# A gated linear attention and token-mixing kernel with its steps issued in another order

## Chip, cores and metric

The kernel runs on one core of one Trainium2 chip, in one launch. The metric is the device time of that core in microseconds (us), and the median over several runs is what counts.

## What is computed

Gated linear attention (batch 4, 8 heads, 768 tokens, head dimension 48) gives x, and a token-mixing layer with 384 channels follows. All is float32.

```python
f = 1.0 / (1.0 + np.exp(-f_logit))
for t in range(S):
    state = f[:, :, t, :, None] * state + np.einsum('bhd,bhe->bhde', k[:, :, t], v[:, :, t])
    y[:, :, t] = np.einsum('bhd,bhde->bhe', q[:, :, t], state)
x = y.transpose(0, 2, 1, 3).reshape(B, S, H * D)

theta = x @ w_theta
zr, zi = x * np.cos(theta), x * np.sin(theta)
y = np.einsum('ts,bsd->btd', w_tok_r, zr) + np.einsum('ts,bsd->btd', w_tok_i, zi)
u = x + y
out = u + np.maximum(u @ w_ch, 0.0)
```

## The kernel before

The 768 tokens of each batch are cut into 6 chunks of 128, so the attention has 24 chunks (numbered 0 to 23 over all batches). The mixing works on 8 groups: a group is one batch and one half (384) of its output tokens. The weights arrive as 64-bit floats in 16 parts and are decoded to float32 on the chip. For batches 1 to 3 each matrix product of the mixing layer is made of three products of split (high and low) operands; batch 0 uses whole float32 operands.

The work is divided into small steps, each a function that issues a few instructions. `ORDER` is one hand-fixed list of 1169 steps, the engines' programs follow it, and every engine runs its own instructions in that order and waits where an operand or a buffer isn't ready. A step code stands for its next number: the third `gk` in the list is `gk` 2. A mark after a slash sends the step's instruction to another engine than its usual one: /A ScalarE, /D VectorE, /P GpSimd. The loop at L608 to L613 reads the list: it counts each code, sets the engine (L612) and calls the function (L613). Since a list entry is the n-th of its code, chunks, parts and groups are always done in the same sequence among themselves; the list sets only how the codes interleave.

The codes, with their line and engine:

- Loads, all issued from SP: `lf`, `lk`, `lq` (gates, keys, queries of a chunk, L555), `lv` (values, L560), `lw` (raw weights of a part, L202, two transfers for most parts). Three buffers each for f, k, q and v: a load waits until the chunk three before has been used.
- Gates of a chunk: `gc` clamp (VectorE or GpSimd, L269), `go` (ScalarE, L274 and L275), `gs` scan (VectorE, L279), `ge` two exponentials (ScalarE, L286 and L287), `gp` (GpSimd, L290), `gq` scale q (VectorE or GpSimd, L294), `gk` scale k (VectorE, L299).
- Attention of a chunk: `sc` scores (TensorE, L333), `ma` mask (VectorE, L339), `ke` transposes of k (TensorE, L347), `kt` copy (ScalarE or VectorE), `up` state update products (TensorE, L362), `sa` and `st` (VectorE, L370 and L374), `sm` (VectorE or GpSimd, L378), `qs` and `ou` output products (TensorE, L393 and L401), `xc` copy of x, `xt` transposes (TensorE, L411), `xs` copy into the output tile u (ScalarE or VectorE). `sc`, `up`, `qs` and `ou` use 64-row tiles of TensorE, all other TensorE steps 128 rows.
- Angles of a chunk: `xh`, `xl` split x (the second on VectorE or GpSimd, L433), `th` (TensorE, L442), `tn`, `se`, `ab` reduce the angle, `tr` sine and cosine (ScalarE, L465 and L466, with a change of its function table), `ro` rotate (VectorE, L475), `zh`, `zl` split the result (L482).
- Weights of a part: `d1` (VectorE, L215), `d2` (ScalarE, L220), `d3` (VectorE, L225 and L226), `di`, `d4`, `d5` (scale and split, the last L250), `e4`, `e5` the same for the channel weights.
- Mixing: `f0`, `f1`, `f2` are the products of one chunk for a third of the channels (TensorE, L498), `v` adds them to u (VectorE, L502), `uh`, `ul` split u (the second L509), `c` channel products (TensorE, L516), `cv` (VectorE, L530), `so` store (SP, L534). The last group's store stands at L690, behind the list.

`PLACES` names, for each kind of tile, the buffer that its n-th tile takes: `a` the two double banks of PSUM, `b` four single banks, `wp` decoded weights, `z` raw weights and rotated chunks, and so on.

## Time and profile before

| | us |
|---|---|
| median of 3 runs | 337.95 |
| lowest and highest of them | 337.77, 339.97 |
| the profiled execution, its own time | 338.16 |
| its span, from the first to the last instruction | 335.5 |

The profile is of one execution. Engines are PE (TensorE matmul), PEld (its weight loads), DVE (VectorE), ACT (ScalarE), POOL (GpSimd) and SP (which issues the transfers). Ends of matmuls are modelled, so the distance between the first weight loads of two steps tells better what a step takes than the busy time. A wait is named by what released it; "issue" means that the profile shows nothing that the engine waited for.

### The profile page before, as it was taken

To read this page: it belongs to the slowest core of one execution; us is meant where nothing else is said; L and a number is where in the kernel's file an instruction comes from. 1 tells how busy PE (TensorE), PEld (TensorE's weight loads), DVE (VectorE), ACT (ScalarE), POOL (GpSimd) and SP (SyncE) were. 2 spreads that over 40 slices of the span, in tenths; PEclk is the share of its full clock that TensorE was granted. 3 is DMA by queue.
4 is the path that set the end of the run, shared out by engine and by line. 5 is a ranking of instruction groups with operands and counts; after the bars stand their busy time and mean duration, and the time that the engine had idled before them with its cause. 6 is when DMAs were issued, how large, how long until landed. Compare 5 with 4: busy or idle time off the path is not lost.

```text
span 335.5 us, 9996 instructions
## 1 busy us (share of the span) xinstructions
PE 316.8 (94%) x4320; PEld 280.7 (84%) x4320; DVE 243.4 (73%) x394; ACT 192.9 (58%) x321; POOL 112.3 (33%) x109
## 2 busy tenths in 40 slices
PE   0798999999999999999999999999999999999993
PEld 0685676567676789999999999999999999999992
DVE  5999999999999899968659777774526677441031
ACT  6789977787696799847468253953805342310010
POOL 2452074318100146265371248143800521103110
PEclk9999999999999999999999999999999999999998
DMA  7989779758660463240405353250122102000022
GB/s 266 395 244 304 254 249 340 249 181 308 243 212 17 150 225 111 91 156 15 130 3 168 115 160 117 88 178 0 33 73 79 49 2 73 0 2 0 0 73 77
DMA packets 21619, 45.54 MB, mean 136 GB/s; under 512 B 2369, under 2 KB 5441, under 8 KB 21569
## 3 DMA queue, kind: packets, MB, share of 16 engines
q1 hardware_dynamic: 21568, 44.84, 39.6%
q8 instruction: 36, 0.59, 0.7%
q14 instruction: 15, 0.11, 0.1%
HBM read 40.11 MB, written 4.72 MB: 134 GB/s over the span
## 4 chain that ended last, share of the span: by engine, by line
PE 83%; DVE 9%; ACT 2%; DMA 2%; issue 2%; DVEq 0%; ACTq 0%
PE pm L498 47%; PE pch L516 10%; PE pth L442 9%; PE wide L401 4%; PE wide L393 3%; PE wide L333 3%; PE pxt L411 2%; PE psk L347 2%; PE wide L362 2%; DVE f L279 2%; DMA out_dram<-ut 1%; DVE z L475 1%; DVE raw L215 1%; DMA f<-in_f_dram 1%; DVE k L299 1%
## 5 line engine op out<-in xcount | busy, mean ns | idle before, releaser
L498 PE MATMUL pm<-wp,z 128*128 128x384 f32 x648 | 117.1, 336 | 0.0
L498 PEld LDWEIGHTS pm<-wp,z 128*128 128x128 f32 x648 | 112.4, 188 | 0.0
L498 PE MATMUL pm<-value,z 128*128 128x384 f32 x144 | 49.3, 487 | 0.2 <-DVE z L475 0.2
L516 PE MATMUL pch<-uhl,wch 128*128 128x384 f32 x216 | 40.2, 339 | 0.4 <-DVE ut L176 0.4
L498 PEld LDWEIGHTS pm<-value,z 128*128 128x128 f32 x144 | 26.3, 190 | 15.9 <-DVE value L226 0.5
L516 PEld LDWEIGHTS pch<-uhl,wch 128*128 128x128 f32 x216 | 37.5, 188 | 1.0 <-DVE ut L176 0.7
L290 POOL COPY pes<-p 128x4 f32<-128x4 f32 x24 | 11.4, 476 | 72.6 <-ACT p L286 68.2
L502 DVE TENSOR_TENSOR ut<-pm,ut 128x384 f32<-128x384 f32 x24 | 13.1, 552 | 29.8 <-PE pm L498 29.8
L176 ACT CAST uhl<-ut 128x384 fp32r<-128x384 f32 x18 | 9.2, 509 | 41.5 <-DVE ut L502 41.5
L279 DVE TENSOR_TENSOR_SCAN f<-carry,f 128x512 f32<-128x512 f32 x24 | 29.1, 1222 | 0.7 <-ACT f L275 0.7
L433 POOL TENSOR_TENSOR xl<-ut,xh 128x384 fp32r<-128x384 f32 x13 | 13.5, 1041 | 46.1 <-DVE xh L176 29.1
L286 ACT ACTIVATE p<-f 128x512 f32<-128x512 f32 x24 | 15.1, 628 | 21.7 <-DVE f L279 21.3
L509 POOL TENSOR_TENSOR uhl<-ut,uhl 128x384 fp32r<-128x384 f32 x13 | 13.5, 1047 | 37.0 <-DVE uhl L176 18.6
L347 PE MATMUL psk<-ident,k 128*128 128x128 f32 (+1 forms) x96 | 16.8, 302 | 8.9 <-DVE k L299 8.8
L269 POOL TENSOR_SCALAR f<-f 128x512 f32<-128x512 f32 x14 | 23.3, 1668 | 1.5 <-DMA f<-in_f_dram 1.5
L530 DVE SCALAR_TENSOR_TENSOR ut<-pch,ut 128x384 f32<-128x384 f32 x24 | 13.0, 553 | 14.7 <-PE pch L516 14.4
L482 POOL TENSOR_TENSOR z<-w,z 128x768 fp32r<-128x768 f32 x9 | 17.4, 1931 | 17.8 <-ACT z L176 9.6
L442 PE MATMUL pth<-wth,xh 128*128 128x384 f32 x108 | 23.0, 348 | 0.0
L299 DVE SCALAR_TENSOR_TENSOR k<-f,k 128x512 f32<-128x512 f32 x24 | 19.5, 813 | 3.7 <-ACT f L287 3.6
L401 PEld LDWEIGHTS wide<-v,sc 64*64 64x64 f32 x768 | 15.0, 140 | 8.1 <-issue 4.7
L347 PEld LDWEIGHTS psk<-ident,k 128*128 128x128 f32 (+1 forms) x96 | 11.9, 148 | 11.6 <-POOL pes L290 8.8
L475 DVE TENSOR_TENSOR w<-w,x 128x768 f32<-128x768 f32 x18 | 18.1, 1010 | 4.0 <-ACT w L466 4.0
(84 smaller groups left out, 607.3 us busy)
## 6 DMA issues: line engine op xcount, KB each, us to landing
v<-in_v_dram SPq DMA_DIRECT2D x24, 384.0 KB, 4.4
f<-in_f_dram SPq DMA_DIRECT2D x24, 256.0 KB, 3.6
k<-in_k_dram SPq DMA_DIRECT2D x24, 256.0 KB, 4.1
q<-in_q_dram SPq DMA_DIRECT2D x24, 256.0 KB, 3.9
raw<-in_w_r_dram SPq DMA_DIRECT2D x12, 384.0 KB, 5.1
raw<-in_w_i_dram SPq DMA_DIRECT2D x12, 384.0 KB, 5.6
out_dram<-ut SPq DMA_DIRECT2D x21, 192.0 KB, 2.4
raw<-in_w_theta_dram SPq DMA_DIRECT2D x3, 384.0 KB, 5.5
```

The source lines that it names most:

```text
L269: on(nc.vector).tensor_scalar(ft, ft, F_MIN, None, op0=ALU.max)
L279: nc.vector.tensor_tensor_scan(fl, carry[:, pairs(h)].rearrange("p n t -> p (n t)"), fl, 0.0, ALU.mult, ALU.add)
L286: nc.scalar.activation(ps_[m][:, pairs(h)], ft, AF.Exp, scale=-1.0)
L299: nc.vector.scalar_tensor_tensor(kt, loaded["f", m][:, pairs(h)], E_TOP, kt, op0=ALU.min, op1=ALU.mult)
L347: nc.tensor.transpose(psks[m][:used(m), p, :], loaded["k", m][:, p, :used(m)], ident)
L401: nc.tensor.matmul(out[HALF[t], j, p, :], scs[m][HALF[a], j, p, :], v2[HALF[a], t, p, :], start=(t == 0 and m % NC == 0 and p == 0), stop= ...
L433: on(nc.vector).tensor_tensor(xls[m], src, xhs[m], op=ALU.subtract)
L442: nc.tensor.matmul(pths[m], l, r, start=(n == 0), stop=(n == len(ms) - 1))
L475: nc.vector.tensor_tensor(zs[m] if full else w, w, xs[m].unsqueeze(1).to_broadcast([P, 2, DM]), op=ALU.mult)
L482: on(nc.vector).tensor_tensor(zs[m][:, 0], ws[m], zs[m][:, 1], op=ALU.subtract)
L498: nc.tensor.matmul(pms[g, d], l, r, start=(s == 0 and i == 0), stop=(s == NC - 1 and i == len(ms) - 1))
L516: nc.tensor.matmul(pcs[g, d], l, r, start=(es[0] == 0 and n == 0), stop=(es[-1] == KD - 1 and n == len(ms) - 1))
```

## The change

Only two tables change. `ORDER` holds the same 1169 steps, code by code, in another sequence, and some steps carry another engine's mark: on VectorE instead of GpSimd two more `gc`, three `d5`, two `xl`, two `zl` and one `sm`; on GpSimd instead of VectorE one more `gq` and one `ul`; on VectorE instead of ScalarE four `tn`, three `kt`, two `xc`, one each of `d4`, `xs` and `uh`; on ScalarE instead of VectorE two `xh`, two `zh` and two `ab`. In `PLACES` the rows `a`, `b`, `wp` and `z` name other buffers; the other rows stay. The new list in full, and of the old one the first twelve lines, three of the middle and the last six:

```diff
 PLACES = {
-    "a": "0110110101001010110101010101010101010101010101010",
-    "b": ("012301230120123023300300002121123222230230203120310202001031023333312312023011203100000023"
-        "1030303030032123123211120303031"),
+    "a": "0110101010110100101010101010110010101010101010101",
+    "b": ("012301230123103202200200003013121111231231202101201202021230130300000321230121202010102131"
+        "3103213131213021021223100313102"),
     "f": "012012012012012012012012",
     "k": "012012012012012012012012",
     "q": "012012012012012012012012",
     "ut": "01201201",
     "v": "012012012012012012012012",
     "w": "010101010101010101010101",
-    "wp": "0123456789abcdefghijklmno013245687cd",
+    "wp": "0123456789abcdefghijklmno012354689gi",
     "x": "012012012012012012012012",
-    "z": "0123450123412342342350421350421350421",
+    "z": "0123450123512351351430512430512430512",
 }
 ORDER = (
-    "lf gc go lf gc go lf gs lk lq gc gs ge gk gq ke go gp lv sc ge gp gs lk lw lq kt lv lf gk d1 lk lw gq/P lf",
-    "up lq sa d2/P ke kt st ge d3 di d4 qs lv up ma gp ou xc lw sm/P sa gk ke st d1 lf d2 gq gc/P go sm/P d5 gs",
-    "qs gc/P d1 kt lk sc up go sa ma st ge gp gk lq lk d3 lv xt xs lf ou xc gq gs di d2/P gc/P ke kt lq xt go d3",
-    "gs th lw gc ge gp tn se lv gq qs gk sc up ma lq d1 xs go gs sm/P ab/A th ge gq ke kt lk gp ou sa st sm xc xt",
-    "gk d2 xs qs d3 sc up lw ge tr ma tn ro se lv ab gp lq ke kt th tn se sa st ou xc f1 xt xs/D lk qs gk sc tr",
-    "up ma sm/P lf lf d1 ab/A tr ro ro/P ke kt/D gc/P gc/P go sa lv th f0 go gs ou xc gq/P sc up lf gs ma qs sa",
-    "st ge lk gk xt gp f0 d4 f1 tn se xs th lq d2/P lw ke kt d3 sm lk gq/P ou xc/D tn ge se lv d1 sc up ma qs",
-    "d2/P xt f1 f2 f2 xs sa lw gc/P d1 ab ab/A d2 d3 d3 lw d1 f2 lw go gs d5/P th tr ro st tn sm/P gp lv lq gk d1",
-    "gq lq se tr d2 lk f0 ab/A f0 f1 ou ke ro f0 lf tr xc qs d3 kt sc up lw lw d1 xt ro/P f0 d2 d3 d2/P xs f1 f1",
-    "f1 d3 gc/P f1 d1 v lq ge d2 lv go lf xh gp gk gq/P sa st v ke ma xl/P ou sc kt up sm/P gs ge xc/D qs xt sa",
-    "st d4 gc/P xs d4/D f2 d4 ma lk gq lw d1 d2 lf gc/P th tn f2 f2 d3 lw d1 go lq gk ke d3 f1 go gs gs f1 uh kt",
-    "f2 se xh gp ge gq gp lw d1 ou xc ul/P v uh ab xl d2 d3 lv ge gp lk sc up ma qs d2 d3 xt lw xs ul tr f0 f2 f2",
...
-    "sc up xc ma gq qs ke kt/D sa f2 f2 ul uh ul/P f1 f0 ro/P v uh lv ul v c c xh/D cv cv lq c cv zh lf ou xc/D",
-    "sc up v ma gp ge sa qs xl/P uh/D uh gp ul ul gc/P go xt gq xt zl/P lk gk th tn se st ab tr lv sm/P c c so so",
-    "so lf xs/D cv gc/P lk c xh/D xl th zl/P xs xh xl/P ro/P ke kt ou xc/D cv sc up qs xt tn zh/D f0 lv se ab/A",
...
-    "xs so ul kt f2 f2 f2 xh/D xl/P th ma ou ro/P ro/P zh xc sc up ma qs zh/D zl/P tn xt f1 xs se xh/D f1 v sm f2",
-    "v zl/P f1 uh/D ul sa xl/P th ou uh xc tn ab/A gq qs sc xt ma ul/P c xs/D se tr ro/P xh/D xl/P c cv so cv c",
-    "zh/D zl cv ou xc/D th xt xs/D tn/D se ab/A tr f2 ro ab/A f0 f0 gp fl f1 f2 f1 zh tr zl ro/P xh xl/P f0 th tn",
-    "se ab/A zh/D zl tr ro f2 f2 zh zl f0 so f1 f0 f1 f1 f1 f0 v uh/D f1 f2 f1 f1 f1 f2 v f2 so v uh/D uh ul/P f0",
-    "f2 f2 f0 f0 f0 f0 f0 v f2 ul/P ul/P c c cv cv so f1 c cv v so so uh uh f2 f2 v ul/P c ul/P uh ul c c rv cv",
-    "cv cv",
+    "lf lf lf gc gc lk go gs lq gc go lk gs ge gk lq gp ke lv lv gq sc go gs lf ge gk gq/P kt up sa st gp sm ge",
+    "gp ke lk gk kt lw d1 qs lq lf lv gc/P up sa ma st gq/P go lf gs ke d2/P gc kt d3 ou sc xc go gs ge lw gp qs",
+    "di d1 lq d4 lk up lk ma sm/P sa gq/P xt xs/D st d2 gk ge ou xc d3 di lq gq sc ke lw gp lf xt gc/P go d1 d2",
+    "gk gc th lv lf qs kt xs gs d3 up ma ke ge go sm/P sa tn th lk st gk se tn ou lv xc sc xt qs sm kt/D up xs/D",
+    "th gs ma ou ab/A lq gq/P lw d1 gp tr ro lf ge lq sa st lv ke d2/P se xc kt/D tn/D f1 ab/A gc/P gq qs lk gk",
+    "lv gp se sc go up ma xt xs sm f0 ab sa tr tr d3 ro/P lw d1 gs ke ro/P kt th lf ou xc d2 tn d3 sc up sa qs xt",
+    "f1 xs lw lw ge ma lk d1 d1 d2 gc/P go st se th gk lq lq ab/A gq lv f0 gs f1 ou tn/D gp xc ke kt qs sc up",
+    "gc/P ge xt se ab/A sm/P sa d3 f2 f2 f2 lw lf lk tr lw ma lq d1 ro f0 lk d2 d3 d1 gq/P d2/P gk lw xs d4 d4 f0",
+    "th f2 gc/P tr ro/P f2 gp st tn/D d2/P se d5 ab/A tr d1 f1 d3 ke d2 ou kt sc lv up sm/P xc qs xt ro/P f0 f0",
+    "go go f1 xs xh xl/P d3 f1 sa d3 gs ge d5/P f2 ma lw d1 gk ke st lv ou d2 kt v d5 d3 xc sc up qs lq lf sm",
+    "gc/P v lw lf xt xs/D f2 gq gp gs d4 lk lw th tn/D f1 d4 d4 d4/D d4 f1 f2 se ma v d1 ge gp f2 d4 lv lk gc gk",
+    "ke xh/D d1 f0 sa st uh go ou sc gq/P kt gs d2/P lw xc up qs d2/P d3 ma xt xl/P d1 f1 lf d3 ge f2 gc/P xs sm",
+    "sa d2 d5 go gs f0 d3 f1 st lw lq ab lw th tn se tr f0 gk lq f2 d1 ab/A ke xh f0 d2/P tr f1 d1 ro/P gq sc gp",
+    "ul kt d3 d2 d3 ou uh lk ro xl f0 ge gq/P zh zh f1 xc/D f0 gk qs lv lv v uh e4 lf lf up ma sm ke zl/P lq sa v",
+    "e4 e5 e5 go ul/P kt th ou xc uh sc up ul tn se lk lk gs qs ab/A d5 gp c ul/P lv sa tr c c cv f2 st so ro/P",
+    "cv cv gc/P go zl v f1 f1 uh ul so so ge xt gp uh gk ke ma gq ou sc kt xc/D d4/D xs xh/D xl up ma d4/D gs qs",
+    "xt xt zh sm ul/P lf xs th tn se xh xl/P d4/D c d5 ab c sa cv st zl xs ge tr c th gp lq gq tn gk xh f1 cv cv",
+    "se ab/A tr f0 f0 ke ro zh/D zl xl/P ro/P so th tn lv kt/D gc/P gc/P f0 ou xc sc lk up so so se ab/A zh zl qs",
+    "d5 d5/P tr sm/P d5 go go gs ge gs xt lq lf ro/P gq/P zh/D zl/P lv lk xs f2 f2 f2 xh xl ma lq gc f0 gp f1 f1",
+    "f0 f2 f2 sa th tn f0 v se ab ou d4 d5/P ge gq xc f1 gp f2 gk ke uh gk go lf f1 f1 st d5 f1 ul/P v v lf kt/D",
+    "qs sm sc up gc gs xt lk ke kt/D uh uh sa st xs ge xh/D xl/P f2 f2 sm/P f2 ma ul/P gc gk go th tn/D ou d5 tr",
+    "lv ul sc up sa lq se gq d4/D xc qs c f0 cv ab gp f1 gs ro lv st ke so ge kt ma zh lk gk f0 f0 f0 c go gp tr",
+    "ou xc/D sc up cv d5/P zl qs d5 xt xs lq f0 f2 lf xh xl lk lq gq/P gc ma lv go c f0 gs ge so cv so f1 sm/P sa",
+    "gp f1 f2 v uh/D ul/P gq v uh gs gk f2 v uh/D ro/P zh/D th tn xt xs/D ke kt zl/P ou xc/D sc up qs xt se xh xl",
+    "ke kt/D ab/A f2 xs th sa tr st tn/D ul/P ul/P c ge lk c ro cv lf lf gk ma cv f2 zh zl/P se ke ou xh xl sc lq",
+    "gp xc lv up qs xt so th ab tr ro xs f0 f0 f0 tn/D xh xl/P se th kt/D zh zl f0 c lv ma ou sm sa st ab/A tr ro",
+    "zh/D sc up tn se xc/D cv qs ab/A so so ma xt xs/D tr ro/P zh/D lq f1 lq zl/P zl lf f1 f1 gc/P f0 sm f1 f1 f2",
+    "f0 go f0 gc gc gq xh xl/P v gs ge gp f2 f2 f1 v f2 f1 lk gk sa go v th go tn/D f1 ke se st ou gq/P xc/D gs",
+    "sm/P sc kt lv up ma qs sa gs xt xs lk ge gq uh gk st sm/P lq lk gp f1 f0 ul f0 f0 f1 ge gq xh/D f0 uh f0 f1",
+    "uh/D v ul/P ab tr uh lv f1 ke ul kt/D ou xc/D sc up qs xl/P v c cv f2 th sa st gk f2 ro so zh f2 zl/P ke tn",
+    "se xt xs/D ab xh xl/P c sm/P c uh cv so ma ou kt tr lv f2 cv f2 so ro/P qs xc sc up ma xt zh/D zl th tn se",
+    "ou xc f2 sa qs xs xh/D sc v uh/D xt ab/A xl/P tr xs th tn ul/P ul/P se f0 ul/P f0 ro/P zh/D zl/P c xh/D xl",
+    "cv c cv ab/A tr th ma ou tn/D se f2 xc xt f1 xs/D f2 f2 xh xl/P ro/P ab/A tr zh zl th tn/D se ab/A gp f2",
+    "ro/P zh zl tr ro f1 f1 f1 f1 f0 zh zl f0 f0 f2 f2 f0 v f1 v f2 c v f0 so f0 f0 f0 uh/D uh/D fl ul ul f0 f0",
+    "cv f2 v f2 f1 so so f1 uh uh/D f1 f2 f2 f2 ul/P c cv c cv f1 f1 f1 ul c v v c uh uh so so cv so ul c ul/P c",
+    "rv cv cv cv",
```

## Rows read from the trace of the kernel before

**Rows 1.** The page, busy time of each engine (share of the span) and instructions.

```profile
PE 316.8 (94%) x4320; PEld 280.7 (84%) x4320; DVE 243.4 (73%) x394; ACT 192.9 (58%) x321; POOL 112.3 (33%) x109
```

**Rows 2.** Busy time by stretches: start:end, length, each engine, granted clock, DMA share, GB/s.

```profile
45.00:112.00 67.00, 66.88 (x937) 45.22 (x936) 65.77 (x101) 51.46 (x86) 19.81 (x19) 1.00 0.67 233
112.00:330.00 218.00, 217.19 (x2710) 210.57 (x2708) 137.67 (x231) 103.94 (x173) 76.03 (x65) 1.00 0.24 76
```

**Rows 3.** In order of time, 0 to 20 us: start, duration, engine, line, what [idle <-releaser].

```profile
3.63 0.43 DVE L269 TENSOR_SCALAR f<-f 128x512 f32<-128x512 f32 x1 [2.03 <-DMA f<-in_f_dram]
...
4.09 1.08 SPq L202 DMA_DIRECT2D raw<-in_w_theta_dram  x2
...
8.72 0.33 SPq L555 DMA_DIRECT2D f<-in_f_dram  x1
8.80 0.71 PEld L347 LDWEIGHTS psk<-ident,k 128*128 128x128 f32 x4 [8.80 <-POOL pes L290]
```

**Rows 4.** The same, 314 to 336 us.

```profile
324.70 4.70 PEld L516 LDWEIGHTS pch<-uhl,wch 128*128 128x128 f32 x27
...
330.46 0.39 SPq L690 DMA_DIRECT2D out_dram<-ut  x1
```

**Rows 5.** The chain that ended last, in order of time: start, us, what.

```profile
72.03 6.45 PE pm L498 x20
...
160.95 10.41 PE pm L498 x60
171.36 1.56 PE pth L442 x9
...
188.94 4.68 PE pch L516 x27
```

**Rows 6.** In order of time, weight loads (PEld) of 117 to 120 us.

```profile
116.83 0.19 PEld L516 LDWEIGHTS pch<-uhl,wch 128*128 128x128 f32 x1
117.27 0.59 PEld L401 LDWEIGHTS wide<-v,sc 64*64 64x64 f32 x32 [0.25 <-issue]
117.73 0.60 PEld L333 LDWEIGHTS wide<-q,k 48*64 48x64 f32 x32
118.20 0.50 PEld L362 LDWEIGHTS wide<-v,ktok 64*48 64x48 f32 x32
...
119.03 0.14 PEld L393 LDWEIGHTS wide<-mid,q 48*64 48x64 f32 x2
119.22 0.42 PEld L347 LDWEIGHTS psk<-ident,k 128*128 128x128 f32 x4
```

**Rows 7.** Waits of the weight loads, 45 to 330 us: total, times, longest.

```profile
PEld wide L401 <- issue: 4.5, 17, 0.5
```

**Rows 8.** In order of time, weight loads near 201 us.

```profile
201.57 1.52 PEld L516 LDWEIGHTS pch<-uhl,wch 128*128 128x128 f32 x9 [0.73 <-DVE ut L176]
```

**Rows 9.** In order of time, VectorE at 84 to 90 us.

```profile
85.97 0.69 DVE L299 SCALAR_TENSOR_TENSOR k<-f,k 128x512 f32<-128x512 f32 x1
86.57 0.95 DVE L225 SCALAR_TENSOR_TENSOR raw<-raw 128x768 int32<-128x768 int32 x1
87.56 0.96 DVE L226 SCALAR_TENSOR_TENSOR value<-raw 128x768 int32<-128x768 int32 x1
```

**Rows 10.** In order of time, weight loads near 88 us.

```profile
88.57 0.62 PEld L498 LDWEIGHTS pm<-value,z 128*128 128x128 f32 x3 [0.47 <-DVE value L226]
```

**Rows 11.** In order of time, VectorE near 34 and near 104 us.

```profile
33.86 0.35 DVE L370 TENSOR_TENSOR mid<-wide,st 128x192 f32<-128x192 f32 x1
...
104.19 0.69 DVE L294 TENSOR_TENSOR q<-q,p 128x512 f32<-128x512 f32 x1
```

**Rows 12.** In order of time, GpSimd and VectorE near 75 us.

```profile
75.12 1.29 POOL L294 TENSOR_TENSOR q<-q,p 128x512 f32<-128x512 f32 x1
75.49 1.47 DVE L299 SCALAR_TENSOR_TENSOR k<-f,k 128x512 f32<-128x512 f32 x1
```

**Rows 13.** DMA issues of the page: KB each, median us to landing.

```profile
raw<-in_w_theta_dram SPq DMA_DIRECT2D x3, 384.0 KB, 5.5
```

15 rows, old and new, of the table ORDER are left out of this document.

## The prediction

> **What bounds the kernel now.** I read the page's busy table first, then the busy time by stretches, then who waited for whom on TensorE, then single stretches in order of time. TensorE is busy 316.8 of 335.5 us and VectorE 243.4 [rows 1]. The stretches say more: from 45 to 112 us both are full (TensorE 66.88 and VectorE 65.77 of 67 us), and from 112 to 330 us TensorE alone is (217.19 of 218, VectorE 137.67), at a granted clock of 1.00, the upper level of 2.4 GHz [rows 2]. So TensorE's work, laid end to end, is the floor, and what an order can change is how much TensorE loses between its first weight load at 8.80 [rows 3] and the start of the last `c` step. The last three `c` start at 324.70 and take 4.70 us [rows 4], so the last starts at 324.70 + 2/3 x 4.70 = 327.83. After it come 335.5 - 327.83 = 7.67 us: the three `cv` and the last store [rows 4].
>
> To know the loss I price each step when nothing holds it. From undisturbed runs: an `f` step of batches 1 to 3 takes 10.41/10 = 1.04 us, an `f` step of batch 0 6.45/5 = 1.29, `c` 4.68/3 = 1.56, `th` of batches 1 to 3 1.53 (1.56, of which the next step gives a few hundredths back) [rows 5]; the attention steps follow each other by .46 (117.27, 117.73, 118.20) [rows 6], `qs` by .50. `ke` (.39), `xt` (.28), `th` of batch 0 (1.73) and the two short forms (`qs` of a batch's first chunk .46, `up` of its last .39) I take from the typical distance of successive first weight loads. A run of attention steps (`sc up qs ou`, 64-row tiles) also costs something at its ends: after the last 128x128 load at 116.83 the next load comes at 117.27, .27 later than the .17 spacing before it, and after the last 48x64 load at 119.03 the transposes begin at 119.22 instead of .04 later, .15 more [rows 6]. In 45 to 330 us the profile books 4.5 us of such pauses to no engine ("issue"), 17 of them ahead of L401 [rows 7]. I take .30 for an entry and .15 for an exit.
>
> Laid out: `sc` 24 x .467, `up` 20 x .467 and 4 x .386, `qs` 20 x .50 and 4 x .46, `ou` 24 x .461, `ke` 24 x .39, `xt` 24 x .28, `th` 6 x 1.73 and 18 x 1.53, `f` 36 x 1.29 and 108 x 1.04, `c` 23 x 1.56, `fl` .1: 293.8 us; 30 entries and 30 exits: 13.5. Together 307.3. TensorE had 327.83 for it from the span's start, so 20.6 are lost: 8.8 before it starts, 10.3 up to 41 us, .4 more by 112 us, 1.1 later (.73 of these at 201.57, behind a VectorE copy into an output tile, which a store had to leave first [rows 8]).
>
> The loss is VectorE's doing. A VectorE instruction in a full queue costs its mean less .09, for the next starts that much before it ends (85.97, 86.57, 87.56: .60 for a row of .69, .99 with a small gap for one of .95) [rows 9]. With such prices I add up, along the program, VectorE's work ahead of a TensorE step, and subtract TensorE's work ahead of it. In the old order the difference is 11.8 us at `qs` 3 (27.2 - 15.4), 8.3 at the `f1` that follows `d3` 11 (77.1 - 68.7) and 7.5 at the first `c` (100.2 - 92.7). To this come VectorE's start at 3.63 [rows 3] and its slippage, the time it idled or was slowed: `d3` 11 ended at 88.52 [rows 9], so 88.52 - 3.63 - 77.1 = 7.8. The sum 8.3 + 3.6 + 7.8 = 19.7 meets what TensorE had lost there, 88.57 - 68.7 = 19.9, and the row shows it waiting for just that instruction, .47 us [rows 10].
>
> **The change part by part.** No arithmetic, transfer or table load is added: 1169 steps in both orders, and 11 changes of ScalarE's table and back in both. Three things move.
>
> *Engines.* `ro` and `d2` steps marked /P are not moved (the mark does nothing there). Over the whole program VectorE gets 9.2 us more and GpSimd 12.5 less, mostly after 112 us, where VectorE idles 80 of 218 us [rows 2]: nothing there, as long as that idle time covers it.
>
> *The start.* Up to the first product (`f1` 0, after `ro` 0) the new order has on VectorE one `d3` (1.86), one `d5` (.87) and three `gq` (1.81) less, and one `gc`, one `kt`, one `sm` and two `xs` (2.16) more: 31.7 becomes 29.3, for the same 20.0 us of TensorE's work. The highest difference falls from 11.8 (`qs` 3) to 9.4 (`up` 4). That is 2.4 us less loss at that point. The first steps, up to `ke` 0, ask the same of VectorE, so TensorE again starts at 8.8.
>
> *What follows it.* Later the new order is worse: the difference is 9.2 at `ke` 7 (45.1 - 35.9), 8.3 at `ke` 9 (68.2 - 59.9) and 7.8 at `ke` 11 (92.3 - 84.5; the old order has 6.0 there). Ahead of `gk` 11 stand two `gc`, two `sm`, four `tn`, two `xs`, two `d5`, one each of `kt`, `xh`, `sa`, `st` more (7.9 us), and three `gq`, two `ul`, two `xc`, one each of `ro`, `xl`, `d4`, `d1`, `ab` less (6.1). With the old slippage at that depth (`gq` 12 ended at 104.88, with 92.9 of work done: 8.4 [rows 11]) `ke` 11 gives 7.8 + 3.6 + 8.4 = 19.8 us of loss: the gain of the start is spent by 105 us. Two more `gq` run on GpSimd by then. A `gq` there that starts at 75.12 is seen beside a `gk` on VectorE of 1.47 us [rows 12], against .69 undisturbed [rows 9]; two such cost 0 to 1.6, and I take .2, for VectorE has other short slack. Loss at `ke` 11: 20.0.
>
> *Entries and exits.* In the new order TensorE's attention steps stand in 34 runs instead of 30 (for instance `qs` 10 and `up` 11 stand apart from `sc` 10 and `ou` 9, `ou` 13 from `qs` 14, `ou` 21 and 22 from what followed them). All four extra runs lie behind `ke` 11, where TensorE has no slack: 4 x (.30 + .15) = 1.8 us. The ends are 0 (the pause hides) and 4 x (.50 + .15) = 2.6 by the longest such pause. The row shows pauses at the ends of a run and none inside it, from L401 to L333 to L362 [rows 6]. The Trainium skill (TensorEngine Tiling (Array Packing), Key Properties) says that changing the tiling mode, not just the tile, drains TensorE; it gives no price. By that rule every extra run costs and the sum is 1.8 higher than without it; the trace agrees, with the .27 and .15 above.
>
> *The queues.* On SP the raw weights of part 0 move from 4.09 to behind the fourth `lf`, which waited until 8.72 [rows 3]: some 5.5 us to landing [rows 13] from 10.0 would be 15.5, and VectorE comes to `d1` 0 at about 14.0 (3.6, 7.7 of work, 2.7 of slippage, a little under what the old order had there). I take no wait, and 1.5 us as the upper end. `lk` 18 stands behind a store that waits for `cv` 6; `ke` 18 comes some 17 us of TensorE work later, which hides its landing. The pair `so` 11, `xs` 18 has the 2.05 us of TensorE work between that cost .73 at 201.57, but 14 `f` follow: I count .6 for all late losses (before: 1.1; ends 0 and 2).
>
> *The tail.* `f1` 47 is followed by two `c` (3.1 us), which cover `v`, `uh` and `ul` of 22 (some 2.9): 7.67 as before.
>
> Sum: TensorE's work 307.3 + 1.8 = 309.1, loss 20.0 + .6, tail 7.67: span 337.3. The profiled execution took 338.16 for its 335.5, so 2.66 lie around it: 340.0. It stood .2 above the median of the runs shown: **339.8**, against 337.95.
>
> **The rivals.** *The gain of the start is kept* (VectorE slips less in 45 to 105 us, since its copies wait less for TensorE): the loss is then set at the start: 9.4 + 3.6, the old slippage there (`sa` 3 ended at 34.21 with 27.2 done: 3.4 [rows 11]), and .8 for one slowed instruction [rows 12]: 17.2, 2.8 less than forecast: 337.0. For it: GpSimd has 27.9 us instead of 28.6 ahead of `gk` 11. Against: the old trace agreed with the sum to .2 us at 88 us.
>
> *The pauses hide*: 1.8 less, 338.0. For it speaks only that they are booked to nothing; against, that they recur ahead of 17 of the L401 runs.
>
> *Slower by over 1%: the weights come late.* Place: `d1` 0 on VectorE. Behind it stand `sa` 1, `ma` 0, `st` 1 and `gs` 3, and for them wait `ou` 0, `qs` 1 and ScalarE's `ge` 3. Each us of wait shifts all later differences, `ke` 11 too, which has no slack: 1.5 us make 341.3, and from there on it decides. For it: the queue is full at 10 to 20 us. Against: the new order asks for fewer bytes before it.
>
> **How the numbers follow.** Forecast .52, gain kept .18, pauses hidden .10, late weights (or another new wait of that size) .20. One per cent, 3.4 us, is what a measurement of this kernel can tell from no change. The forecast's own 338.4 to 341.3 and the first two rivals lie within it; the third beyond 341.3 with .16, and faster than 334.6 needs the two first together and no late loss: .04. The range 336.8 to 342.6 leaves out .06 below and .12 above.
>
> **What would show it.** Right: `ke` 11 waits for `gk` 11 near 104 us; TensorE ahead of the old trace by 1 to 2 us at `f1` 0 (near 38 us) and level with it at 105; L401 and L393 with four more pauses booked to "issue"; 7.7 us from the last `c`. Wrong: TensorE still ahead at 112 us, or a VectorE wait for a raw tile's transfer near 14 us.

## The result, and the profile after

The changed order takes 339.22 us (median of 11 runs, 338.60 to 340.32) where the order before takes 337.40 (11 runs, 336.65 to 339.97): a ratio of 1.0051, 95% interval 1.003 to 1.0072. That is 1.8 us slower, and within one per cent. The profiled execution took 338.6 us with a span of 336.9 (before: 335.5).

Within the span the change costs more than the time says. In the eleven executions of the changed order 1.7 to 1.8 us of the time lie outside the span; in 19 executions of the order before, taken with the first experiments, it is 2.05 to 3.05, 2.6 in the median. Their median spans are 337.5 and 335.2, 2.3 us apart. Why less time lies outside the span isn't shown; the versions that are made from the order after share its 1.7 to 1.9.

The page of the order after, busy time of each engine (beside [rows 1]), and its busy time by stretches (beside [rows 2]):

```profile
PE 318.6 (95%) x4320; PEld 280.6 (83%) x4320; DVE 254.3 (75%) x408; ACT 191.2 (57%) x315; POOL 98.6 (29%) x101
```

```profile
45.00:112.00 67.00, 66.45 (x887) 44.33 (x886) 66.17 (x99) 52.33 (x85) 16.40 (x17) 1.00 0.65 226
112.00:330.00 218.00, 218.00 (x2753) 210.60 (x2752) 148.65 (x242) 102.21 (x173) 63.89 (x59) 1.00 0.24 78
```

VectorE has 10.9 us more and GpSimd 13.7 less, nearly all of it after 112 us, where VectorE still idles 69 of 218 us. TensorE has no idle time left there, and finishes later.

In order of time, 0 to 20 us (VectorE, SP's queue, TensorE's weight loads; beside [rows 3]):

```profile
3.32 0.43 DVE L269 TENSOR_SCALAR f<-f 128x512 f32<-128x512 f32 x1 [1.72 <-DMA f<-in_f_dram]
...
8.49 0.72 PEld L347 LDWEIGHTS psk<-ident,k 128*128 128x128 f32 x4 [8.49 <-POOL pes L290]
...
9.25 0.91 SPq L202 DMA_DIRECT2D raw<-in_w_theta_dram  x2
...
15.64 0.57 DVE L215 TENSOR_SCALAR raw<-raw 128x768 int32<-128x768 int32 x1 [1.58 <-DMA raw<-in_w_theta_dram]
```

Everything starts .3 us earlier than before, since the first gates happened to land earlier (3.32 against 3.63; nothing ahead of them was changed). The raw weights of part 0 are issued at 9.25, behind the fourth `lf`, and VectorE stands still 1.58 us for them at `d1` 0. This was the wait that the prediction held for possible and counted at nothing.

Around `ke` 11, in order of time:

```profile
103.82 0.68 DVE L299 SCALAR_TENSOR_TENSOR k<-f,k 128x512 f32<-128x512 f32 x1
...
104.55 0.39 PEld L347 LDWEIGHTS psk<-ident,k 128*64 128x64 f32 x4 [0.40 <-DVE k L299]
```

`gk` 11 ends at 104.50 and TensorE, which waited .40 for it, starts `ke` 11 at 104.55. The work ahead of it is worth 84.5 us by the prediction's prices, so 20.05 are lost by then, where 20.0 were forecast.

The tail (beside [rows 4]):

```profile
324.68 6.28 PEld L516 LDWEIGHTS pch<-uhl,wch 128*128 128x128 f32 x36
...
332.07 0.39 SPq L690 DMA_DIRECT2D out_dram<-ut  x1
```

The last of four `c` starts at 329.4 (before: 327.8), and 7.5 us follow.

To compare executions that did not start at the same moment I count below from the first weight load (8.49 after, 8.80 before; it lay between 8.49 and 9.20 in all profiles, also where nothing ahead of it was changed). So counted, in us, in the one profiled execution of each version:

| | `f1` 0 | `ke` 11 | last `c` | time, us | ratio to the order before |
|---|---|---|---|---|---|
| before | 30.46 | 95.23 | 319.02 | 337.4 to 338.0 | |
| after | 30.09 | 96.06 | 320.89 | 339.22 | 1.0051 [1.003, 1.0072] |
| nine runs split (from before) | 30.09 | 96.60 | 323.89 | 342.73 | 1.0131 [1.0097, 1.0165] |
| twelve pauses added (from before) | 30.24 | 95.01 | 328.97 | 347.27 | 1.0281 [1.0242, 1.032] |
| four runs joined (from after) | 30.34 | 95.63 | 325.42 | 343.89 | 1.017 [1.0127, 1.0213] |
| `lw` 0 earlier (from after) | 30.06 | 95.27 | 320.12 | 338.17 | 1.002 [0.9994, 1.0046] |
| `lk` 2 and `lw` 0 earlier (from after) | 30.95 | 96.25 | 321.07 | 339.20 | 1.0028 [1.0002, 1.0055] |
| four `tn` on ScalarE (from after) | 30.15 | 96.12 | 321.99 | 340.45 | 1.0085 [1.0056, 1.0115] |
| early scans cut (from before) | 29.88 | 95.05 | 318.13 | 337.57 | 0.9989 [0.9968, 1.001] |
| early scans cut (from after) | 29.29 | 94.54 | 319.76 | 338.62 | 1.0022 [0.9999, 1.0046] |
| later scans cut (from after) | 29.89 | 94.92 | 321.29 | 340.21 | 1.0063 [1.004, 1.0086] |
| ScalarE cut (from before) | 31.80 | 97.32 | 320.64 | 338.23 | 0.9996 [0.9975, 1.0017] |
| both cut (from before) | 29.61 | 94.82 | 318.22 | 337.38 | 0.9969 [0.9947, 0.9991] |
| both cut (from after) | 29.31 | 94.55 | 319.37 | 338.79 | 1.0025 [1.0, 1.0051] |

The table also shows what one execution is worth. The order before, "twelve pauses added" and "nine runs split" are the same program up to `f1` 0 and have it at 30.46, 30.24 and 30.09; the order after, "four runs joined" and "later scans cut" at 30.09, 30.34 and 29.89. So a difference of .4 us at `f1` 0 can be chance, and between the two orders none is shown there. The ratio of a version made from the order after holds the .9 us by which its time outside the span is shorter.

### The profile page after: what moved, and what is told of

The parts are those of the page before. It is cut to its first block, busy times and chain, and to the rows that moved or that the text cites. A ratio compares the mean times of both kernels' runs of the same rounds, so it can differ in the third digit from the quotient of the medians.

```text
span 336.9 us, 10017 instructions
## 1 busy us (share of the span) xinstructions
PE 318.6 (95%) x4320; PEld 280.6 (83%) x4320; DVE 254.3 (75%) x408; ACT 191.2 (57%) x315; POOL 98.6 (29%) x101
## 5 line engine op out<-in xcount | busy, mean ns | idle before, releaser
L498 PE MATMUL pm<-wp,z 128*128 128x384 f32 x648 | 119.4, 338 | 0.0
L176 ACT CAST uhl<-ut 128x384 fp32r<-128x384 f32 x17 | 8.5, 507 | 36.3 <-DVE ut L502 26.5
L509 POOL TENSOR_TENSOR uhl<-ut,uhl 128x384 fp32r<-128x384 f32 x14 | 15.9, 1143 | 45.0 <-ACT uhl L176 44.0
L433 POOL TENSOR_TENSOR xl<-ut,xh 128x384 fp32r<-128x384 f32 x11 | 11.6, 1056 | 51.5 <-ACT xh L176 29.1
L294 POOL TENSOR_TENSOR q<-q,p 128x512 f32<-128x512 f32 x10 | 14.7, 1474 | 36.5 <-DVE w L475 15.2
L290 POOL COPY pes<-p 128x4 f32<-128x4 f32 x24 | 9.0, 374 | 51.1 <-ACT p L286 47.8
L269 POOL TENSOR_SCALAR f<-f 128x512 f32<-128x512 f32 x12 | 21.9, 1826 | 1.0 <-DMA f<-in_f_dram 1.0
L299 DVE SCALAR_TENSOR_TENSOR k<-f,k 128x512 f32<-128x512 f32 x24 | 20.2, 845 | 1.7 <-ACT f L287 0.8
L482 POOL TENSOR_TENSOR z<-w,z 128x768 fp32r<-128x768 f32 x7 | 13.6, 1941 | 25.7 <-ACT z L176 13.5
```

The costliest lines, as they stand in the source:

```text
L269: on(nc.vector).tensor_scalar(ft, ft, F_MIN, None, op0=ALU.max)
L294: on(nc.vector).tensor_tensor(qt, qt, ps_[m][:, pairs(h)], op=ALU.mult)
L299: nc.vector.scalar_tensor_tensor(kt, loaded["f", m][:, pairs(h)], E_TOP, kt, op0=ALU.min, op1=ALU.mult)
L482: on(nc.vector).tensor_tensor(zs[m][:, 0], ws[m], zs[m][:, 1], op=ALU.subtract)
L498: nc.tensor.matmul(pms[g, d], l, r, start=(s == 0 and i == 0), stop=(s == NC - 1 and i == len(ms) - 1))
L509: on(nc.vector).tensor_tensor(us[g, d][:, 0], uts[g][:, d, :], us[g, d][:, 1], op=ALU.subtract)
```

## The experiments

**What does a split of an attention run cost?** Three runs ask. The first joins four of the runs in the order after, so that 30 remain; one of the four moves (numbers added to the codes):

```diff
-ab12 ou13 d412 d59/P ge16 gq16 xc13 f117 ... kt15/D qs14 sm12 sc14 up15
+ab12 d412 d59/P ge16 gq16 f117 ... kt15/D ou13 sc14 xc13 up15 qs14 sm12
```

> The new order with its four extra runs of attention steps joined to their neighbours again: the three f steps between ou 9 and qs 10 now stand ahead of the run, ou 13 moves next to sc 14, the f steps between ou 21 and qs 22 and between ou 22 and qs 23 stand behind the run. TensorE has 30 runs instead of 34; no step changes its engine. If a run's ends cost about .45 us (theory of the pauses): 1.8 us less, of which up to .5 goes to waits for the output bank that ou 9 and ou 22 must leave first, so 1.3 to 1.8 us less than the new order: span 335.1 to 335.6, ratio to the kernel before about 1.000 to 1.001. If the pauses hide and the loss is only VectorE's (rival): span 336.9, ratio 1.005.

Measured: 343.89 us, slower than either order. By the prices the work fell by 1.8 us, but 6.3 more were lost. Weight loads of this run, in order of time, with what each waited for:

```profile
113.00 0.14 PEld L393 LDWEIGHTS wide<-st,q 48*64 48x64 f32 x2 [0.34 <-DVE x L176]
...
163.99 0.42 PEld L347 LDWEIGHTS psk<-ident,k 128*128 128x128 f32 x4 [1.75 <-DVE k L299]
...
269.45 0.44 PEld L362 LDWEIGHTS wide<-v,ktok 64*48 64x48 f32 x16 [0.98 <-DMA v<-in_v_dram]
...
275.70 0.56 PEld L333 LDWEIGHTS wide<-q,k 48*64 48x64 f32 x32 [0.98 <-DVE mid L370]
```

Steps that had stood a few products apart now wait for each other's copies: `qs` 10 for the copy `xc` 9 out of the bank that `ou` 9 had filled, `sc` 23 for VectorE, `up` 23 for a load, `ke` 15 for `gk` 15. What stood in between was the cover of these waits. This run shows that the order after could not have had fewer of them just so.

The second takes the order before and splits six runs twice, twelve pauses more:

```diff
-ou14 xc14 sc15 up16 tr13 qs15 sm13/P xt14 f021 lk18 f022
+ou14 f221 xc14 sc15 f122 up16 tr13 qs15 sm13/P xt14 ...
```

> The old order with twelve runs more: in six late runs (ou 12, 14, 15, 18, 19, 21 and what follows) the last f step ahead of the run moves to between sc and up, and the one ahead of it to between ou and sc; nothing else moves. 42 runs instead of 30, all extra ones behind 135 us, where TensorE is full. Theory of the pauses: 12 x .42 to .45 = 5.0 to 5.4 us more: span 340.5 to 340.9, ratio 1.015 to 1.016. Rival, pauses hide: span 335.5, ratio 1.000. In between, by .27 (only the entries cost): 338.7, ratio 1.010.

Measured: 347.27 us, last `c` 9.95 later, far more than expected. Here too new waits came on top, about half of the 9.95 (`ke` 20 alone waited 1.21 us for VectorE): a product ahead of `sc` delays `sc`, and everything of that chunk behind it. Neither run tells the price of a pause.

The third puts a product only where nothing hangs on the delay, between `up` and `qs`, in nine runs of the order before:

```diff
-ou14 xc14 sc15 up16 tr13 qs15 sm13/P xt14 f021
+ou14 xc14 sc15 up16 tr13 f021 qs15 sm13/P xt14
```

> The order before, with one product step pulled forward into each of nine runs of attention steps: it now stands between `up` and `qs` instead of behind the run, so only that `qs` and the steps between come about 1 us later, and no `sc`, `up` or `ou` comes earlier or later by order. Nine runs more (39). Theory (an entry and an exit cost .30 + .15 us of TensorE, which has no slack): 9 x .45 = 4.0 us, 341.8 where the order before is at 337.8, and around each of the nine the trace shows an f followed by the first load of `qs` .27 to .30 later than its own spacing, and the `up` before it followed by the f's load .15 late. Rival (the pauses hide): 337.8 to 338.2. Second rival (as in the run with twelve, new waits come on top): over 342.5.

Measured: 342.73 us. Weight loads of one of the nine, in order of time:

```profile
180.68 0.50 PEld L362 LDWEIGHTS wide<-v,ktok 64*48 64x48 f32 x32
181.23 1.01 PEld L498 LDWEIGHTS pm<-wp,z 128*128 128x128 f32 x6
182.50 0.14 PEld L393 LDWEIGHTS wide<-st,q 48*64 48x64 f32 x2 [0.26 <-issue]
...
183.11 0.31 PEld L411 LDWEIGHTS pxt<-ident,x 128*128 128x128 f32 x3
```

and the same `up` 16 and `xt` 14 in the order before:

```profile
177.94 0.50 PEld L362 LDWEIGHTS wide<-v,ktok 64*48 64x48 f32 x32
...
178.97 0.31 PEld L411 LDWEIGHTS pxt<-ident,x 128*128 128x128 f32 x3
```

From `up` to `xt` it takes 183.11 - 180.68 = 2.43 us. In the order before, `xt` 14 follows 1.03 after `up` 16, and the product took .99 from one first load to the next in its old place: 2.02. The split costs .41. Four others with a product of the same form give .40 to .43 in the same way; the fifth, behind `up` 17, gives .23, since the order before already took 1.21 there. The three of batch 0 take 2.65 or 2.66; less the distance before (1.02, 1.02, 1.23) and the 1.29 of such a product, that is .34 twice and .14. The nine make some 3.1 of the 4.87 us by which the last `c` came later; 1.1 of the rest is a new wait of `ke` 10 (1.84) less the .73 at [rows 8], which was not there this time. What is left, some .7, isn't traced. So the pause is real and it costs TensorE: the rival by which it hides is out, and new waits came on top, as the second rival had it. The four extra runs of the order after are worth 4 x .41 = 1.6 us; 1.8 were forecast.

The orders themselves bear this out. From `ke` 11 to the last `c` TensorE has the same work in both, in 15 runs before and in 19 after. That stretch takes 223.1 to 223.8 us in the four profiles of the order before in which nothing behind `ke` 11 was changed, and 224.8 to 225.2 in five of the order after, 1.0 to 2.1 us more. (Two more of the order after, in which `ke` 12 came late, are treated below.)

**Did the late weights eat the start's gain?** In the order after, `lw` 0 is moved ahead of the fourth `lf`:

```diff
-go gs lf ge gk gq/P kt up sa st gp sm ge gp ke lk gk kt lw d1
+go gs lw lf ge gk gq/P kt up sa st gp sm ge gp ke lk gk kt d1
```

> The new order with one step moved: lw 0, the transfer of the first raw weights, stands ahead of the fourth lf, so that it is issued near 5 us and not behind the wait for gk 0. In the new kernel VectorE waits 1.58 us for it at d1 0. Theory that VectorE's queue carries a delay on to ke 11 (loss 20.0 us there): all later VectorE work comes 1.6 us earlier, the loss ends 1.2 to 1.6 us lower, span 335.3 to 335.7, ratio 1.000 to 1.002. Rival, the start has other waits of the same size behind this one (ma 0, ma 1, ScalarE) or VectorE is slowed more: span 336.5 to 337, ratio 1.004 to 1.005.

Then, so that the keys of chunk 2 aren't pushed back by it, `lk` 2 too:

```diff
-go gs lf ge gk gq/P kt up sa st gp sm ge gp ke lk gk kt lw d1
+go gs lk lw lf ge gk gq/P kt up sa st gp sm ge gp ke gk kt d1
```

> The order after, with the loads `lk` 2 and then `lw` 0 both ahead of the fourth `lf` on SP, so that neither the raw weights of part 0 (awaited 1.6 us by VectorE in the order after) nor the keys of chunk 2 (awaited .9 us when `lw` 0 alone was moved) come late. Nothing else differs. Theory (transfers ate the gain of the start): `f1` 0 1.2 to 1.8 us earlier than 38.6. Rival (other waits stand right behind, ScalarE's above all): less than .8 us, as in the run with `lw` 0 alone; 338.0 to 338.8 in time.

Measured: 338.17 and 339.20 us. VectorE with the first edit, in order of time:

```profile
14.35 0.69 DVE L299 SCALAR_TENSOR_TENSOR k<-f,k 128x512 f32<-128x512 f32 x1 [0.89 <-DMA k<-in_k_dram]
...
34.57 0.56 DVE L176 COPY ut<-pxt 128x384 f32<-128x384 f32 x1 [0.92 <-PE pxt L411]
```

The 1.58 us are gone, and .89 for the keys and .92 for TensorE have come: `f1` 0 stands at 30.06 from the first load, as in the order after. With both loads earlier neither of these two transfers is awaited, and `f1` 0 comes .86 *later*. VectorE in that run, in order of time:

```profile
17.93 1.23 DVE L279 TENSOR_TENSOR_SCAN f<-carry,f 128x512 f32<-128x512 f32 x1 [1.03 <-ACT f L275]
...
35.92 2.19 DVE L279 TENSOR_TENSOR_SCAN f<-carry,f 128x512 f32<-128x512 f32 x1
```

The fourth `lf`, which now stands behind the two loads, takes 5.80 us to land instead of 3.77. GpSimd's `gc` 3 and ScalarE's `go` 3 come late for it, and VectorE waits 1.03 us at `gs` 3, which starts 8.73 us from the first load, as in the order after (8.76): the gain at `d1` 0 is spent four steps later, on another transfer. Behind it `xs` 2 comes .31 later than in the order after, since `th` 0 ran for longer at TensorE's lower clock level, and `gs` 6 takes 2.19 us, beside a `gq` and a `gp` on GpSimd, instead of 1.22.

TensorE's weight loads in that run, and the granted clock (the column before the last two) by stretches:

```profile
23.37 0.98 PEld L401 LDWEIGHTS wide<-v,sc 64*64 64x64 f32 x32 [2.49 <-DVE sc L339]
```

```profile
20.00:22.00 2.00, 1.13 (x55) 0.83 (x47) 1.97 (x3) 1.94 (x5) 0.62 (x1) 1.00 0.51 174
22.00:24.00 2.00, 0.63 (x24) 0.63 (x26) 2.00 (x6) 1.97 (x3) 2.00 (x3) 0.54 1.01 343
24.00:26.00 2.00, 2.00 (x54) 1.80 (x49) 1.97 (x5) 1.66 (x4) 1.27 (x3) 0.50 0.41 160
```

TensorE waited 2.49 us for `ma` 1; in 20 to 24 us it was busy 1.76 of 4, and from 22 to 29 us it was granted .50, the lower level of 1.2 GHz. So late transfers are a part of what ate the start's gain, but to issue one earlier makes another late, and does not give the gain back.

**Is VectorE's work what holds the start?** The prediction put all of the loss there. The scans `gs` of chunks 3, 4 and 5 are cut to a quarter of their columns, some 2.4 us of VectorE work ahead of `f1` 0, in the order before and in the order after:

```diff
+        cl = carry[:, pairs(h)].rearrange("p n t -> p (n t)")
+        if m in (3, 4, 5):
+            fl, cl = fl[:, :C], cl[:, :C]
-        nc.vector.tensor_tensor_scan(fl, carry[:, pairs(h)]..., fl, 0.0, ALU.mult, ALU.add)
+        nc.vector.tensor_tensor_scan(fl, cl, fl, 0.0, ALU.mult, ALU.add)
```

> The order before; the gate scans of chunks 3, 4 and 5 (VectorE) run over one of their four column groups only, so the gates of the other three are left without their sums. Nothing else differs; some 2.4 us of VectorE work (3 x .8) fall away ahead of `f1` 0. Theory (what VectorE has to do ahead of a TensorE step, plus a start and a slippage that stay, sets what TensorE loses): all that follows comes 2.4 us earlier: `f1` 0 at 36.9 instead of 39.3, and the time 335.4 where the order before is at 337.8. Rival (the start is set by something else as well: TensorE on its lower clock level up to some 25 us, ScalarE, transfers; VectorE then idles longer): f1 0 earlier by less than 1.2 us, 336.6 or more.

> The order after, with the same three scans cut to a quarter (the gates of the other column groups are left without their sums). Theory (VectorE's work sets the loss): 2.4 us earlier at `f1` 0 (36.2 instead of 38.6) and at `ke` 11, 336.8 where the order after is at 339.2. Rival (the start after is held by the weights' transfer and by TensorE on its lower clock level until 27.6 us): less than 1.2 us earlier at `f1` 0; what the whole gains may then still be more, since `ke` 11 stands behind it.

Measured: 337.57 us in the order before, no difference; `f1` 0 only .58 earlier (.21 against the earliest of the three profiles that share this start). In the order after, 338.62 us, `f1` 0 .80 earlier (.60), and the last `c` 1.1. VectorE's waits of 8 to 40 us in the order before with the cut (engine, line, waited for: us, times, longest):

```profile
DVE k L302 <- ACT f L290: 0.7, 2, 0.4
DVE w L456 <- ACT w L450: 0.6, 1, 0.6
DVE mid L371 <- PE wide L365: 0.5, 1, 0.5
DVE raw L225 <- ACT raw L220: 0.4, 1, 0.4
```

VectorE, with less to do, came to stand for ScalarE (1.7 us of these) and for TensorE. In the order after, the same cut ended in transfers: 1.11 us at `d1` 0 and 1.27 at `d1` 2, each for a raw tile. The theory of 2.4 us falls in both.

Then ScalarE alone, and both together, in the order before; and both in the order after. ScalarE's second exponential of chunks 1 to 6 is cut to a quarter:

```diff
+        if m in (1, 2, 3, 4, 5, 6):
+            ft = ft[:, :1]
         nc.scalar.activation(ft, ft, AF.Exp)
```

> The order before; ScalarE's second exponential of the gates of chunks 1 to 6 runs over one of four column groups (the other three keep their sums in place of exponentials). About 6 x .4 = 2.4 us of ScalarE's work fall away ahead of `f1` 0, and VectorE keeps all of its own. In the run with VectorE's scans cut, VectorE came to wait 1.7 us for ScalarE, and `f1` 0 came .6 us earlier only. Theory now (ScalarE, full from 16 to 39 us, and VectorE hold the start between them, so that neither alone gives much): `f1` 0 by .3 to 1 us earlier than 39.3. Rival (ScalarE alone holds it): 2 us or more earlier, 335.9 or less where the order before is at 337.9. Second rival (neither: TensorE on its lower clock level, or transfers): no change.

> The order before, with both cuts: the second exponentials of chunks 1 to 6 and the scans of chunks 3, 4 and 5 over a quarter of the columns (the others are left out). 2.4 us less on each of the two engines ahead of `f1` 0. Theory (both hold the start together): `f1` 0 1.5 to 2.4 us earlier than 39.3, and since all later differences of VectorE fall too, 335.5 to 336.4 where the order before is at 337.9. Rival (TensorE's own start holds it: its lower clock level up to 25.7 us in the order before, and what it waits for in a circle with the two): 1 us or less, 336.9 or more.

> The order after, with the same two cuts. Theory (both engines hold the start together): `f1` 0 1.5 to 2.4 us earlier than 38.6, and since `ke` 11 behind it has no slack but loses the same VectorE work, 336.8 to 337.7 where the order after is at 339.2. Rival (the transfer of the raw weights, awaited at 15.6 us, and TensorE's lower clock level until 27.6 us hold it): less than 1 us at `f1` 0.

Measured: with ScalarE cut, 338.23 us, no difference. The profiled execution was the slowest of its twelve (339.60), and in it `f1` 0 came 1.34 us later. By stretches, and weight loads of `th` 2, in this run:

```profile
32.00:34.00 2.00, 0.99 (x21) 0.57 (x13) 1.54 (x2) 1.83 (x4) 0.96 (x1) 1.00 1.03 344
34.00:36.00 2.00, 1.55 (x92) 1.55 (x92) 1.78 (x6) 1.73 (x3) 0.32 (x1) 0.87 0.76 298
36.00:38.00 2.00, 2.00 (x17) 1.48 (x10) 1.97 (x4) 1.99 (x5) 0.00 (x0) 0.50 0.55 144
```

```profile
37.68 0.33 PEld L444 LDWEIGHTS pth<-value,ut 128*128 128x128 f32 x1 [0.31 <-issue]
38.32 0.33 PEld L444 LDWEIGHTS pth<-value,ut 128*128 128x128 f32 x1 [0.31 <-issue]
```

TensorE was busy .99 of 2 us in 32 to 34, and fell to the lower level in 35 to 39 us: each product of `th` then takes .64 from load to load, where an undisturbed `th` of batch 0 takes 1.73 for six, .29 each. Here TensorE itself is late: VectorE's `ro` 0, whose result `f1` 0 takes, ended 1.3 us before `f1` 0 started.

With both cut, 337.38 us before (`f1` 0 .85 earlier) and 338.79 after (.78 earlier): both times my theory of two engines falls as well; the rivals (1 us or less at `f1` 0) have the size right. In the order after with both cuts, VectorE's waits in 8 to 40 us begin with

```profile
DVE raw L215 <- DMA raw<-in_w_i_dram: 1.9, 2, 1.1
DVE raw L215 <- DMA raw<-in_w_theta_dram: 1.4, 1, 1.4
```

so there transfers take back 3.3 us of what VectorE was spared. No cut of 2.4 or 4.8 us brought `f1` 0 forward by more than .85.

**Is `ke` 11 the one place that decides, and does VectorE's work set it?** First the four `tn` that the change put on VectorE ahead of it go back to ScalarE (`tn/D` becomes `tn` for `tn` 2, 4, 5, 6):

> The new order with tn 2, 4, 5 and 6 on ScalarE again, as in the old order: 2.4 us less on VectorE and 1.5 us more on ScalarE ahead of gk 9 to gk 11. If VectorE's work ahead of ke 9 and ke 11 sets the loss there (20.1 and 20.0 us): it falls by 1 to 1.6 us, down to what ke 7 and f0 3 leave (19.5) and less one tn ahead of these, span 335.4 to 336.1, ratio 1.000 to 1.002. If the loss is set before 40 us (rival): span 336.9, ratio 1.005. If ScalarE is what is late (second rival): span 337.5 or more.

Then the scans of chunks 8, 9 and 10 are cut as above, in the order after:

> The order after, with the scans of chunks 8, 9 and 10 cut to a quarter instead (the gates of the other column groups are left without their sums): 2.4 us less VectorE work between `f1` 0 and `gk` 11, none before. Theory (TensorE's loss is the largest of several points: 18.7 us at `f1` 0, 19.5 at `ke` 7 and f0 3, 20.1 at `ke` 9 and `ke` 11): the loss can only fall from 20.1 to that at the points ahead of the cut, 19.5, or to 18.7 where those also come earlier: 337.8 to 338.6 where the order after is at 339.2. Rival (the work between sets it alone): 2.4 us, 336.8. Second rival (as with the four reductions on ScalarE, VectorE idles or is slowed by as much more): 339 and over.

Measured: 340.45 and 340.21 us, no gain over the order after (339.22; the intervals overlap), and in the profiled executions the last `c` came 1.1 and .4 us later. With the `tn` moved, VectorE was 1.2 us ahead of the order after at `se` 5, but at `gk` 10 it waited .8 us for ScalarE, which had the `tn` again, and took 1.33 us instead of .69 (the second rival: ScalarE is what is late); `ke` 11 stays where it was (96.12 from the first load). With the scans cut `ke` 11 comes 1.14 earlier, but by `ke` 12 1.0 of that is lost, and at the first `c` TensorE is .4 behind the order after. GpSimd and VectorE of the run with the scans cut, in order of time:

```profile
109.62 1.69 POOL L297 TENSOR_TENSOR q<-q,p 128x512 f32<-128x512 f32 x1 [14.75 <-ACT p L289]
110.09 1.64 DVE L436 TENSOR_TENSOR xl<-ut,xh 128x384 fp32r<-128x384 f32 x1
111.26 2.15 POOL L485 TENSOR_TENSOR z<-w,z 128x768 fp32r<-128x768 f32 x1
112.12 1.85 DVE L302 SCALAR_TENSOR_TENSOR k<-f,k 128x512 f32<-128x512 f32 x1
```

and the same two VectorE instructions in the order after, where GpSimd's `gq` 12 starts at 110.98:

```profile
110.89 0.55 DVE L433 TENSOR_TENSOR xl<-ut,xh 128x384 fp32r<-128x384 f32 x1
...
111.83 1.30 DVE L299 SCALAR_TENSOR_TENSOR k<-f,k 128x512 f32<-128x512 f32 x1
```

With the cut, GpSimd is .47 us ahead of `xl` 2, which then takes 1.64 us instead of .55 and ends .42 after GpSimd's instruction does (111.73 against 111.31); `gk` 12 takes 1.85 and ends .56 after GpSimd's next (113.97 against 113.41). In the order after, `xl` 2 is ahead by .09 and takes its .55. The run with `tn` on ScalarE shows the same pair, 1.63 and 1.85. So `ke` 11 is where TensorE last waits for long in the order after, and the end goes with it where nothing else comes late: with the early scans cut it comes 1.5 us earlier and the last `c` 1.1, with `lw` 0 earlier both .8. But `ke` 12 stands right behind it, and what VectorE gains before can be taken back there by who starts first.

## Why the prediction was right, and where it was not

The time came out at 339.22 where 339.8 was forecast, in the range and within one per cent. By its own steps:

- **Work laid out.** 307.3 for the order before and 309.1 for the order after: with these prices, TensorE loses .3 us between `ke` 11 and the last `c` in the order after (forecast .6) and 1.05 in the order before (1.1), so they hold. The extra 1.8 is confirmed in kind, at .41 a run instead of .45.
- **`ke` 11.** 20.05 us lost there, against 20.0 from 7.8 + 3.6 + 8.4 + .2. The parts hold too: VectorE started at 3.32 (forecast 3.6), it idled 4.3 and was slowed 4.5 us (8.8, forecast 8.4 + .2), and the rest up to 104.50 is 92.4 of work (92.3). That the slippage of the old order, 8.4, carries over was assumed without a reason, and the two experiments on `ke` 11 show that it can change by a microsecond with who meets GpSimd first; that it came out so near is in part luck.
- **Tail.** 7.5 us, forecast 7.7.
- **The time around the span.** "2.66 lie around it" was carried over from the order before; it is 1.7 to 1.8 in every execution of the new order. The sum up to there, a span of 337.3, meets the median span of 337.5; that the time came out .6 us below the forecast is due to this term, which was .9 too large.
- **The extra pauses in the waits' view.** Four more pauses booked to "issue", a sign that the prediction named, is not what the view shows:

```profile
PEld wide L401 <- issue: 3.6, 14, 0.5
PEld wide L393 <- issue: 1.2, 4, 0.5
```

  These are 18 together, against 17 [rows 7] and 1. Several of the pauses are put down to an instruction that ended just then (at 116.07, .25 us are put down to a VectorE `v` that `ou` doesn't read). Distances of loads show the pauses, that view doesn't count them.
- **The start, the step that failed.** "That is 2.4 us less loss at that point": from the span's start `f1` 0 lost 18.6 us after and 19.3 before, .7 less (38.59 against 39.26), where "TensorE ahead of the old trace by 1 to 2 us" was forecast. Half of the .7 is the earlier first gates, and the other half, .37, is no more than profiles of one program differ by. The term was the fall of the highest difference in VectorE's work, with VectorE's idle and slowed time held constant. That time was 3.5 us before and 5.4 after at `ro` 0: the gain went into the 1.58 us for the weights and .3 for another raw tile. The assumption behind it, that the loss is VectorE's alone, doesn't hold, as the cuts show. TensorE's waits in 8 to 40 us of the order before, which were there to be read:

```profile
PEld wide L401 <- DVE sc L339: 2.5, 3, 1.0
PEld wide L393 <- DVE st L374: 0.7, 1, 0.7
PEld pxt L411 <- ACT x L176: 0.7, 1, 0.7
```

  Only some 3.6 of the 10.3 us that TensorE lost there are booked to VectorE, some 2.3 to other engines and 1.6 to "issue". The remaining 2.8 are no wait: TensorE's steps took longer, at its lower level. Loads of the order before ([rows 3] is the first of its kind), of the run with twelve pauses added, and of the order after, with the busy time by stretches of the last:

```profile
23.63 0.71 PEld L347 LDWEIGHTS psk<-ident,k 128*128 128x128 f32 x4
```

```profile
22.97 0.42 PEld L347 LDWEIGHTS psk<-ident,k 128*128 128x128 f32 x4 [0.33 <-PE wide L401]
...
28.92 1.59 PEld L442 LDWEIGHTS pth<-value,ut 128*128 128x128 f32 x6 [1.70 <-ACT ut L176]
```

```profile
22.86 0.59 PEld L401 LDWEIGHTS wide<-v,sc 64*64 64x64 f32 x32 [1.88 <-DVE sc L339]
...
24.77 0.71 PEld L347 LDWEIGHTS psk<-ident,k 128*128 128x128 f32 x4
...
27.61 0.89 PEld L442 LDWEIGHTS pth<-value,ut 128*128 128x128 f32 x3 [0.31 <-issue]
30.01 0.42 PEld L347 LDWEIGHTS psk<-ident,k 128*128 128x128 f32 x4
```

```profile
20.00:24.00 4.00, 1.99 (x71) 1.56 (x64) 4.00 (x8) 3.64 (x7) 2.93 (x3) 1.00 0.78 210
24.00:28.00 4.00, 4.00 (x43) 3.06 (x44) 3.97 (x7) 3.49 (x7) 2.35 (x3) 0.57 0.83 307
```

  The transposes of `ke` take .71 at the lower level and .42 at the upper. In the order before the rise falls into `th` 0, near 25.7. In the order after TensorE was at the upper level by 22.86 (`ou` 1 takes .59, at the lower level .98); it had waited 1.88 us for `ma` 1 behind the 1.58 us, was busy 2.0 of 4 us in 20 to 24 (before: 3.5), and then fell: the granted clock is .57 on average over 24 to 28, and the loads are at their upper pace again from near 27.6. From `th` 0 to `qs` 2, the same work, the order after takes 2.93 us, the order before 2.46, and the run with twelve pauses added 2.14.

  But in the order before the lower level isn't what makes `f1` 0 late. The run with twelve pauses added is the same program up to there; TensorE was at the upper level in it by 22.97, and `qs` 2 stands 1.29 us earlier from the first load. It then waited 1.70 us at `th` 1 for ScalarE's copy `xs` 1, where the order before waits .6, and `f1` 0 came only .22 earlier.
- **Late weights.** The third rival was right in its place (`d1` 0, near 14 us, 1.58 us) and wrong in its price: "each us of wait shifts all later differences". Taking the wait away brings `ke` 11 and the last `c` .8 us earlier, half of the 1.58; the waits of .89 and .92 stood right behind it.
- **Gain kept, pauses hidden.** Neither happened.

So the forecast of the end was right because the end is set at `ke` 11 and by the extra pauses, both rightly priced, and the mis-sized start doesn't enter that sum.

What stays open: which of the two copy engines, the transfers and TensorE's lower level would have to give way first at the start. In the order before, a rise some 3 us earlier or more was worth .2 to .4 us at `f1` 0, no more than chance. With `lw` 0 earlier the level may weigh more: `th` 0 to `qs` 2 takes 3.56 us there, and VectorE's .92 us of waiting for TensorE follow. No run held TensorE at its upper level from its first step. That VectorE's work ahead of `gk` 11 sets `ke` 11 is shown where that work or its waits fell at the start; neither of the two runs that took work off VectorE right ahead of it gained at the end. No version beat the order before beyond the interval, save the one that leaves work out on two engines (0.9969).

## What to carry to other kernels

A sum of one engine's work ahead of a step bounds that step only if the waits named for that engine explain the loss; read first which releasers the waits of that stretch name, and whether the same instruction takes its usual time there. Count how often the tensor engine changes between kinds of tiles: each change has a price even where no wait is shown, but joining runs also takes away the cover of the waits that stood between them. Where several engines are full at once, a saving on one of them is mostly lost at the next handover. Before a difference between two profiles is read as an effect, see by how much two profiles of the same program differ there.
